# Attention and two MLPs on one core: q's sum and parts of the third and later head pairs tied to units 3 to 6 of the pair in front

## The chip, the cores and the metric

One core of a Trainium2 chip. The metric is device time of one execution in microseconds (us). Engines are named as in the profile: PE (TensorE matmul), PEld (its weight load), DVE (VectorE), ACT (ScalarE), POOL (GpSimd), SP (SyncE, which issues the DMAs). Each engine takes its instructions in the order in which they were laid down when the kernel was built. An instruction that waits holds up all that stand behind it on its engine.

## The reference

```python
# q, k, v: [4, 8, 576, 64] float32
def rotate(x):
    x1, x2 = (x[..., :half], x[..., half:])
    return np.concatenate([x1 * cos - x2 * sin, x1 * sin + x2 * cos], axis=-1)
q_rot, k_rot = (rotate(q), rotate(k))
scores = (1 / sqrt(64)) * np.matmul(q_rot, k_rot.transpose(0, 1, 3, 2))
scores = scores - np.max(scores, axis=-1, keepdims=True)
attn = np.exp(scores)
attn = attn / (np.sum(attn, axis=-1, keepdims=True) + 1e-09)
x = np.matmul(attn, v)               # turned to [2304, 512]
h = x @ w_in                         # [2304, 2048]
g = np.where(h >= 1, h, np.where(h <= -1, 0.0, (h + 1) ** 2 / 4))
x = g @ w_out                        # [2304, 512]
h = x @ moe2_w_in
out = (s * np.maximum(h, 0) ** 2 + b) @ moe2_w_out
```

## The kernel before

The four batches of eight heads are worked as 16 pairs of heads, counted here from 0 as in the code: pair i, i = 0 to 15. So the third pair of the title is pair 2. A pair has nine units, k = 0 to 8 (`UNITS`): eight are 128 query rows of one head, and unit 4 holds the last 64 rows of both heads. "Unit i.k" below is unit k of pair i, and n = 9i + k.

Numbers in full precision are multiplied as two parts, a high one that PE takes as it is and a low one that is what is left. For scores the high and low part of a head of q are stacked in the 128 rows of one tile (`qs`), and multiplied with two tiles of k, `kh` and `kz`.

One unit goes through the engines like this. PE makes the scores (`sc`, line 357), DVE takes the maximum of each row (`nm`, line 359), ACT takes the exponential and its sum (`p`, line 364), PE transposes it (`tp`, line 379), ACT or DVE copies that out of PSUM (`pt`, lines 382 to 386), and PE multiplies with v (`av`, line 405). There are two score buffers, so that PE can be two units ahead of the exponentials. `eb` (line 422, POOL) holds the inverses of the sums, which PE transposes (`rm`, line 433) and DVE multiplies in (`u`, line 441).

A pair's q needs five steps first: a load into a `qkin` tile (four of these, shared by q and k), a product with a table of cosines and sines on POOL (`pool_tt`, four pieces, line 96), a sum of its two halves on DVE (line 294), and then for each of the two heads the high part on ACT (line 308) and the low part on DVE (line 309). They end in `qs_t[i % 2]`, which the pair two in front has used. k goes the same way, with its sum on POOL, and is brought to `kh` and `kz` by six small DMAs (lines 326 and 329).

Beside the units run two more streams. The weights of the MLPs come in eight bytes a number and are converted on the chip, a half slice at a time, in one chain through ACT, DVE and POOL with one buffer for each step (`convert`: `wa` line 134, `wm` line 135, `wa` lines 137 and 138, `w` line 139, then two subtractions and two additions on POOL, line 96). From n = 48 on the first MLP of finished batches fills PE between the units (`run_fill`, the products `h` and `y`, line 181). What follows attention (the rest of the first MLP, then the second) is bound by PE.

The order on each engine is made when the kernel is built, by a scheduler that takes what is ready in the order of the program; `tc.issue_after(x)` keeps an instruction behind x. In `do_load`, q of pair i + 1 is asked for in unit i.0 as a whole, with no such tie from the third pair on. So its steps go as soon as their tiles are free and their data there, up to two pairs ahead. `maxs[n]` and `exps[n]` are the maximum and the exponential of unit n.

Of the kernel before, what the change touches and what calls it, by code (L numbers as in the profile page):

```python
# [14 lines left out]
ALU = mybir.AluOpType  # L15
# [51 lines left out]
def kernel(ctx, tc, qq, kk, vv, tab, ww1, ww2, s, b, out):  # L67
    nc = tc.nc
# [16 lines left out]
    def pool_tt(out, in0, in1, op, dim=-1):  # L85

        n = out.shape[dim]
        free = 1
        for x in out.shape[1:]:
            free *= x  # L90
        k = min(n, -(-free // PW))
        for i in range(k):
            c = [slice(None)] * len(out.shape)
            c[dim] = slice(n * i // k, n * (i + 1) // k)
            c = tuple(c)
            m = nc.gpsimd.tensor_tensor(out=out[c], in0=in0[c], in1=in1[c], op=op)  # L96
        return m
# [15 lines left out]
    exps, tps, maxs = {}, {}, {}  # L113

    class Slice:
# [6 lines left out]
        def convert(self, raw, pools, hi, lo):  # L122
            if not wide:
                split(hi, lo, raw, nc.scalar, nc.gpsimd)
                return


            top = raw.bitcast(F32).rearrange("p (n t) -> p n t", t=2)[:, :, 1]
            low = raw.bitcast(U16).rearrange("p (n t) -> p n t", t=4)[:, :, 1]
            pool = pools[self.f * 2 + self.made & 1 if len(pools) > 1 else 0]  # L130
            a = pool.tile([P, HW], F32, tag="wa", name="wa", bufs=WB)
            m = pool.tile([P, HW], F32, tag="wm", name="wm", bufs=WB)
            au, mu = a.bitcast(U32), m.bitcast(U32)
            nc.scalar.activation(a, top, AF.Copy, scale=2.0 ** -112)
            nc.vector.tensor_scalar(out=mu, in0=au, scalar1=3, scalar2=None, op0=ALU.logical_shift_left)
            nc.vector.scalar_tensor_tensor(out=mu, in0=au, scalar=0x80000000, in1=mu, op0=ALU.bitwise_and, op1=ALU.bitwise_or)
            nc.vector.tensor_scalar(out=au, in0=mu, scalar1=0xFF800000, scalar2=None, op0=ALU.bitwise_and)
            nc.vector.scalar_tensor_tensor(out=a, in0=low, scalar=2.0 ** -36, in1=a, op0=ALU.mult, op1=ALU.mult)
            nc.scalar.copy(hi, m)  # L139
            pool_tt(out=m, in0=m, in1=hi, op=ALU.subtract)  # L140
            pool_tt(out=lo, in0=m, in1=a, op=ALU.add)
# [106 lines left out]
    tab_sb = att.tile([P, 2, S], F32, name="tab_sb")  # L248
# [4 lines left out]
    qk_in, v_in, stacks = {}, {}, {}  # L253

    WHOLE = [slice(0, S)]
    HALVES = [slice(0, 288), slice(288, S)]

    def load_qk(i, nm, pieces=WHOLE):
        bb, hp = divmod(i, NP)
        t = att2.tile([P, 2, S], F32, tag="qkin", name=f"{nm}in", bufs=QB)  # L260
        for c in pieces:
            nc.sync.dma_start(out=t[:, :, c], in_=(qq if nm == "q" else kk)[bb, hp, :, :, c])
        qk_in[nm, i] = t

    def load_v(i):
        bb, hp = divmod(i, NP)
        t = att2.tile([P, 5, 2, D], F32, tag="vin", name="vin", bufs=VB)
        for out, src in ((t[:, :, 1], vv[bb, hp, :, :, 1]), (t[:D, :4, 0], vv[bb, hp, D:, :4, 0]), (t[D:, :4, 0], vv[bb, hp, :D, 1:, 0]), (t[D:, 4, 0], vv[bb, hp, :D, 0, 0])):
            nc.sync.dma_start(out=out, in_=src)
        v_in[i] = t  # L270
# [15 lines left out]
    def rope_pair(i, nm, mul, add, lo_eng, pieces=WHOLE):  # L286

        t = qk_in[nm, i]
        tt = {nc.gpsimd: pool_tt, nc.vector: nc.vector.tensor_tensor}
        last = None  # L290
        for c in pieces:
            tt[mul](out=t[:, :, c], in0=t[:, :, c], in1=tab_sb[:, :, c], op=ALU.mult)
            r = t[:, 1, c]
            tt[add](out=r, in0=t[:, 0, c], in1=r, op=ALU.add)
            last = (lay_q if nm == "q" else lay_k)(i, t, c, lo_eng)
        return last

    SELF = [slice(0, D), slice(D, P)]
    laid, parts = set(), {}

    def lay_q(i, t, c, lo_eng, heads=range(2)):

        st = stacks["q", i] = qs_t[i % 2]
        r = t[:, 1, c]
        for j in heads:
            own, other = SELF[j], SELF[1 - j]
            at = slice(j * QW + c.start, j * QW + c.stop)
            h = nc.scalar.activation(st[own, at], r[own], AF.Copy, scale=0.125)
            m = nc.vector.scalar_tensor_tensor(out=st[other, at], in0=r[own], scalar=0.125, in1=st[own, at], op0=ALU.mult, op1=ALU.subtract)
        return h.ins, m.ins  # L310
# [218 lines left out]
    def turned_by(t, c):  # L529
        nc.vector.tensor_tensor(out=t[:, :, c], in0=t[:, :, c], in1=tab_sb[:, :, c], op=ALU.mult)  # L530
        return nc.vector.tensor_tensor(out=t[:, 1, c], in0=t[:, 0, c], in1=t[:, 1, c], op=ALU.add).ins
# [53 lines left out]
    def do_load(n):  # L585
        if n == 0:
            with tc.issue_after(turned):
                turned_by(tq, QP[1])
                lay_q(0, tq, QP[1], None)
        elif n in (1, 2):  # L590
            with tc.issue_after(maxs[n]):
                if n == 1:
                    turned_by(tq, QP[2])
                else:
                    lay_q(0, tq, QP[2], None)
        if n < len(units):
            i, k = units[n]
            if i + 1 < NPAIR:
                if i == 0 and k in (2, 6):
                    with tc.issue_after(maxs[k]):  # L600
                        turned_by(qk_in["q", 1], HALVES[k // 6])
                if i == 0 and k in (4, 5, 7, 8):
                    with tc.issue_after(maxs[k]), tc.issue_after(exps[k - 1]):
                        lay_q(1, qk_in["q", 1], HALVES[k // 6], None, [int(k in (5, 8))])
                if i and k == 0:
                    with ExitStack() if i > 1 else tc.issue_after(parts[1][1]), ExitStack() if i > 1 else tc.issue_after(maxs[9]):
                        rope_pair(i + 1, "q", nc.gpsimd, nc.vector, None)
                elif k == 2:
                    with ExitStack() if i else tc.issue_after(exps[2]), ExitStack() if i else tc.issue_after(lowest):
                        rope_pair(i + 1, "k", nc.gpsimd, nc.gpsimd, [nc.gpsimd, nc.vector])  # L610
                elif k == 7:
                    load_v(i + 1)
                elif k in (4, 6) and i + 2 < NPAIR:
                    load_qk(i + 2, "q" if k == 4 else "k")

        if n in range(33, 51, 2) or n in range(70, 110, 4):
            with tc.issue_after(exps[n - 14]):
                convert()

        if n in PARK_AT and parking:  # L620
            with tc.issue_after(exps[n - 4]):
                parking.pop(0).park(wst, scratch)()
# [31 lines left out]
    def do_fill(n):  # L654
        if n < 48:
            return
        with tc.issue_after(exps[min(n, len(units)) - 4]):
            run_fill(0.62 if n < 76 else 0.92)

    acts = {"q": do_qk, "l": do_load, "t": do_t, "a": do_av, "f": do_fill}  # L660
    for n in range(len(units) + LA):
        with ExitStack() as st:
# [541 lines left out]
```

## Time and profile before

| | us |
|---|---|
| median of 3 runs | 1116.61 (1113.03 to 1118.2) |
| the profiled execution | 1117.65, its span 1115.9 |
| PE busy in the span | 1074.3 (96%) |
| DVE busy | 775.0 (69%) |
| ACT busy | 631.0 (57%) |
| POOL busy | 426.9 (38%) |

Attention lies between 9.08 us, where the first scores start, and 417 us, where the last maximum is taken. The shares are those of the whole span. In the first 140 us DVE and POOL are busy more than 80% of the time, so the shares of the attention stage, pair by pair, tell more.

### The profile page before, as it was taken

To read this page: it belongs to the slowest core of one execution; us is meant where nothing else is said; L and a number is where in the kernel's file an instruction comes from. 1 tells how busy PE (TensorE), PEld (TensorE's weight loads), DVE (VectorE), ACT (ScalarE), POOL (GpSimd) and SP (SyncE) were. 2 spreads that over 40 slices of the span, in tenths; PEclk is the share of its full clock that TensorE was granted. 3 is DMA by queue.
4 is the path that set the end of the run, shared out by engine and by line. 5 is a ranking of instruction groups with operands and counts; after the bars stand their busy time and mean duration, and the time that the engine had idled before them with its cause. 6 is when DMAs were issued, how large, how long until landed. Compare 5 with 4: busy or idle time off the path is not lost.

```text
span 1115.9 us, 20052 instructions
## 1 busy us (share of the span) xinstructions
PE 1074.3 (96%) x7296; PEld 981.3 (88%) x7296; DVE 775.0 (69%) x1445; ACT 631.0 (57%) x1440; POOL 426.9 (38%) x564
## 2 busy tenths in 40 slices
PE   5899999989999999999999999999999999999998
PEld 3666788878888889999999999999999999999997
DVE  7888987768576663454757667866777778677754
ACT  5777776766666665454545455474554448334431
POOL 6998977686473332332544445110212110000000
PEclk9999999999999999999999999999999999999999
DMA  8665856656675544655465673231322853221221
GB/s 240 168 191 167 253 160 208 207 165 188 202 227 166 174 151 138 220 171 190 149 183 203 211 238 116 86 112 59 113 89 90 301 171 116 82 83 42 80 63 36
DMA packets 109762, 173.24 MB, mean 155 GB/s; under 512 B 29408, under 2 KB 80608, under 8 KB 109664
## 3 DMA queue, kind: packets, MB, share of 16 engines
q1 hardware_dynamic: 109664, 171.97, 49.1%
q8 instruction: 57, 0.93, 0.4%
q14 instruction: 41, 0.34, 0.1%
HBM read 110.10 MB, written 48.56 MB: 142 GB/s over the span
## 4 chain that ended last, share of the span: by engine, by line
PE 81%; DVE 5%; DMA 5%; POOL 3%; ACT 3%; issue 2%; SPq 0%; POOLq 0%; ACTq 0%
PE hps L181 15%; PE sum L940 14%; PE yps L856 6%; PE yps L855 6%; PE yps L854 6%; PE y L181 5%; PE sc L357 5%; PE yps L790 4%; PE yps L791 4%; PE yps L792 4%; PE av L405 4%; PE h L181 4%; PE tp L379 3%; DMA wraw<-in_ww 1%; DMA kz<-kin 1%
## 5 line engine op out<-in xcount | busy, mean ns | idle before, releaser
L181 PE MATMUL hps<-xh,w 128*128 128x288 f32 (+4 forms) x640 | 163.4, 324 | 0.0
L357 PE MATMUL sc<-kh,qs 128*128 128x288 f32 x336 | 102.7, 328 | 24.5 <-ACT p L364 13.5
L359 DVE TENSOR_REDUCE nm<-sc 128x1 f32<-128x576 f32 x144 | 106.5, 748 | 24.9 <-PE sc L357 24.4
L364 ACT ACTIVATE p<-sc,nm 128x576 f32<-128x576 f32 x144 | 106.7, 742 | 28.6 <-DVE nm L359 26.2
L948 ACT ACTIVATE four<-four,b_sb,s_sb 128x480 f32<-128x480 f32 x64 | 47.4, 782 | 127.2 <-DVE four L947 127.2
L856 PE MATMUL yps<-gh,w 128*128 128x480 f32 (+1 forms) x320 | 118.5, 370 | 0.0
L854 PE MATMUL yps<-gh,w 128*128 128x480 f32 (+1 forms) x320 | 118.4, 370 | 0.0
L855 PE MATMUL yps<-gl,w 128*128 128x480 f32 (+1 forms) x320 | 118.4, 370 | 0.0
L96 POOL TENSOR_TENSOR wm<-wm,w 128x256 f32<-128x256 f32 x80 | 69.5, 888 | 119.1 <-ACT w L139 62.5
L181 PEld LDWEIGHTS hps<-xh,w 128*128 128x128 f32 x640 | 113.2, 188 | 1.0
L357 PEld LDWEIGHTS sc<-kh,qs 128*128 128x128 f32 x336 | 63.5, 192 | 45.7 <-ACT p L364 27.0
L181 PE MATMUL hps<-xl,w 128*128 128x288 f32 (+4 forms) x320 | 103.7, 324 | 0.0
L790 PE MATMUL yps<-gh,w 128*128 128x288 f32 (+3 forms) x288 | 93.2, 324 | 1.4 <-DVE yp L797 0.7
L357 PE MATMUL sc<-kz,qs 128*128 128x288 f32 x336 | 93.8, 301 | 0.0
L791 PE MATMUL yps<-gl,w 128*128 128x288 f32 (+3 forms) x288 | 92.8, 322 | 0.0
L792 PE MATMUL yps<-gh,w 128*128 128x288 f32 (+3 forms) x288 | 92.8, 322 | 0.0
L379 PE MATMUL tp<-ident,p 128*128 128x128 f32 x576 | 87.2, 276 | 4.0 <-DVE pt L386 3.4
L96 POOL TENSOR_TENSOR wm<-wm,raw 128x256 f32<-128x256 f32 x16 | 12.6, 806 | 176.8 <-ACT raw L139 176.8
L181 PE MATMUL y<-gh,w 128*128 128x288 f32 x320 | 75.0, 305 | 2.0 <-DVE ptr L397 0.9
L379 PEld LDWEIGHTS tp<-ident,p 128*128 128x128 f32 x576 | 70.5, 142 | 6.2 <-DVE pt L386 4.1
L405 PE MATMUL av<-pt,vin 128*64 128x256 f32 (+1 forms) x512 | 75.7, 417 | 0.0
L107 DVE TENSOR_TENSOR gl<-hps,gh 128x288 fp32r<-128x288 f32 (+4 forms) x88 | 46.4, 527 | 40.4 <-ACT gh L103 40.2
(154 smaller groups left out, 2905.9 us busy)
## 6 DMA issues: line engine op xcount, KB each, us to landing
wraw<-in_ww SPq DMA_DIRECT2D x56, 512.0 KB, 4.4
w<-parkd SPq DMA_DIRECT2D x24, 512.0 KB, 6.1
kin<-in_k SPq DMA_DIRECT2D x15, 576.0 KB, 4.4
qin<-in_q SPq DMA_DIRECT2D x15, 576.0 KB, 4.8
kh<-kin SPq DMA_DIRECT2D x60, 144.0 KB, 2.9
parkd<-wraw SPq DMA_DIRECT2D x16, 512.0 KB, 3.2
xs<-y1d SPq DMA_DIRECT2D x32, 240.0 KB, 2.7
xd<-u SPq DMA_DIRECT2D x16, 288.0 KB, 2.7
```

The costliest lines, as they stand in the source:

```text
L181: m = nc.tensor.matmul(out_ps, l, r, start=(i == 0), stop=(i == n - 1))
L357: nc.tensor.matmul(sc[:, half, o:o + n], l, r[:, k0:k0 + n], start=m == 0, stop=m == len(todo) - 1)
L364: exps[i * 9 + k] = nc.scalar.activation(p, sc[:, :, :288], AF.Exp, bias=nm, scale=1.0, accum_out=sums_t[i][:, col:col + 1]).ins
L379: m = nc.tensor.transpose(v[:, c, :], p[:, c * P:(c + 1) * P], ident)
L405: nc.tensor.matmul(ps[j * D:(j + 1) * D, :n], v[:, kt, j, :], pt[g][:, kt, j, :], start=kt == 0, stop=False)
L790: nc.tensor.matmul(acc, wh, gh, start=f == 0, stop=False)
L791: nc.tensor.matmul(acc, wh, gl, start=False, stop=False)
L792: nc.tensor.matmul(acc, wl, gh, start=False, stop=last)
L854: nc.tensor.matmul(acc, wh, gh, start=f == 0, stop=False)
L855: nc.tensor.matmul(acc, wh, gl, start=False, stop=False)
L856: nc.tensor.matmul(acc, wl, gh, start=False, stop=last)
L940: nc.tensor.matmul(acc, l, r, start=j == 0, stop=j == len(t) - 1)
```

## The change

From the third pair on, q is no longer prepared in one piece from unit i.0. The product on POOL stays at unit i.0 of the program, now without a tie. The sum on DVE comes at unit i.4, behind the maximum of unit i.3. The high and low part of the first head come at unit i.5, those of the second at i.6, each behind the maximum of the unit in front and the exponential of the unit before that. No instruction is added or taken away.

```diff
+                if i:
+                    t = qk_in["q", i + 1]
+                    if k == 0:
+                        with ExitStack() if i > 1 else tc.issue_after(parts[1][1]):
+                            pool_tt(out=t, in0=t, in1=tab_sb, op=ALU.mult)
+                    elif k == 4:
+                        with tc.issue_after(maxs[n - 1]):
+                            nc.vector.tensor_tensor(out=t[:, 1], in0=t[:, 0], in1=t[:, 1], op=ALU.add)
+                    elif k in (5, 6):
+                        with tc.issue_after(maxs[n - 1]), tc.issue_after(exps[n - 2]):
+                            lay_q(i + 1, t, WHOLE[0], None, [k - 5])
                 if i and k == 0:
-                    with ExitStack() if i > 1 else tc.issue_after(parts[1][1]), ExitStack() if i > 1 else tc.issue_after(maxs[9]):
-                        rope_pair(i + 1, "q", nc.gpsimd, nc.vector, None)
+                    pass
```

The scheduler makes another order on every engine in the attention stage from this. Three places are shown.

The first is DVE from the second maximum of pair 1 to its third and fourth. `qs_107` takes the low parts of pair 2; the second sum is that of pair 3. Before:

```order
L359 TENSOR_REDUCE nm<-sc 128x1
L386 COPY pt<-tp 128x4x128
L309 SCALAR_TENSOR_TENSOR qs_107<-qin,qs_107 64x576 x2
L294 TENSOR_TENSOR qin<-qin 128x576
L359 TENSOR_REDUCE nm<-sc 128x1
```

The same engine after, from the fourth maximum of pair 1 to the seventh:

```order
L359 TENSOR_REDUCE nm<-sc 128x1
L612 TENSOR_TENSOR qin<-qin 128x576
L386 COPY pt<-tp 128x4x128
L359 TENSOR_REDUCE nm<-sc 128x1
L309 SCALAR_TENSOR_TENSOR qs_107<-qin,qs_107 64x576
L359 TENSOR_REDUCE nm<-sc 128x1
L386 COPY pt<-tp 128x4x128
L309 SCALAR_TENSOR_TENSOR qs_107<-qin,qs_107 64x576
L420 RECIPROCAL sume<-sume 128x5
L359 TENSOR_REDUCE nm<-sc 128x1
```

Both low parts of pair 2 and the sum of pair 3 stood between two maxima. Now each step stands between two maxima of its own, and pair 3's sum stands in pair 2. In every later pair too, from 1 to 14, there is one sum behind the fourth maximum and one low part behind each of the next two. Before, pair 1 held two pairs' parts less one step and most later pairs held a sum for the pair three on and the low parts for the pair two on.

The second place is POOL at the second inverse of pair 2 (`eb`), where the second weight conversion (`wm_1084`, `w_1080`) is finished. `qin_1269` before and `qin_1265` after are q of pair 6, `kin_1327` is k of pair 6, `kin_1014` k of pair 5. Before:

```order
L422 COPY eb_882<-sume_879 128x256
L96 TENSOR_TENSOR wm_1084<-wm_1084,w_1080 128x256 x2
L96 TENSOR_TENSOR qin_1269<-qin_1269,tab_sb_106 128x2x144 x4
L96 TENSOR_TENSOR w_1080<-wm_1084,wa_1083 128x256
L96 TENSOR_TENSOR kin_1327<-kin_1327,tab_sb_106 128x2x144 x4
L96 TENSOR_TENSOR w_1080<-wm_1084,wa_1083 128x256
```

After:

```order
L96 TENSOR_TENSOR w_1080<-wm_1084,wa_1083 128x256 x2
L96 TENSOR_TENSOR kin_1014<-kin_1014 128x288 x2
L96 TENSOR_TENSOR qin_1265<-qin_1265,tab_sb_106 128x2x144 x4
L275 MEMSET vin_1056 64x64
L422 COPY eb_1045<-sume_1042 128x256
L275 MEMSET vin_1056 64x64
L96 TENSOR_TENSOR wm_1137<-wm_1137,w_1133 128x256 x2
L96 TENSOR_TENSOR w_1133<-wm_1137,wa_1136 128x256 x2
L96 TENSOR_TENSOR kin_1327<-kin_1327,tab_sb_106 128x2x144 x4
```

The conversion's last two additions stood behind the products of q and of k; now they stand in front of both, and the product of q is directly ahead of the first inverse of pair 3.

The third place is SP at the DMAs that bring k of pair 5 (`kin_1014`) to `kh` and `kz`. Before:

```order
L326 DMA kh_1199<-kin_1014 64x576 x4
L329 DMA kz1_110<-kin_1014 64x576 x2
L262 DMA qin_1595<-in_q 128x1152
L262 DMA kin_1641<-in_k 128x1152
L145 DMA wraw_1288<-in_ww1 128x512
```

After:

```order
L326 DMA kh_1194<-kin_1014 64x576 x4
L329 DMA kz1_110<-kin_1014 64x576 x2
L145 DMA wraw_1286<-in_ww1 128x512
L471 DMA xs_1564<-xd_57 128x288
L262 DMA qin_1591<-in_q 128x1152
```

The load of q for pair 7 (`qin_1595`, now `qin_1591`) stands a little further behind `kz`, and k's (`kin_1641`) went from directly behind it to the end of the same pair. Their tiles are swapped as well: because q's tile is given back later, q of pair i + 2 now takes the tile that k of pair i had (it waits for the DMAs that read it), and k takes q's.

## Rows read from the trace of the kernel before

**Rows 1.** Pairs 1, 2, 6, 9, all: length; busy PE, PEld, DVE, ACT, POOL; clock, DMA.
```profile
33.10:53.50 20.40, 17.31 (x125) 11.78 (x123) 17.75 (x27) 14.90 (x36) 18.63 (x24) 1.00 0.62 176
53.50:71.90 18.40, 18.08 (x133) 12.88 (x132) 16.02 (x28) 13.77 (x34) 16.54 (x21) 1.00 0.67 189
...
132.10:157.90 25.80, 23.24 (x168) 20.93 (x168) 20.73 (x37) 19.50 (x50) 22.11 (x31) 0.93 0.44 131
...
214.50:241.80 27.30, 23.55 (x182) 20.72 (x182) 20.16 (x37) 18.55 (x47) 20.21 (x28) 1.00 0.54 172
...
sum 384.00, PE 361.89 PEld 302.77 DVE 290.87 ACT 271.63 POOL 257.25; mean PE 24.13 PEld 20.18 DVE 19.39 ACT 18.11 POOL 17.15
```

**Rows 2.** Timeline of PE: start, duration, instruction, idle time before it and its releaser.
```profile
36.57 0.66 PE L379 MATMUL tp<-ident,p 128*128 128x128 f32 x4 [1.03 <-DVE pt L386]
...
41.42 0.40 PE L357 MATMUL sc<-kh,qs 128*128 128x288 f32 x1 [1.69 <-ACT p L364]
...
72.81 0.40 PE L357 MATMUL sc<-kh,qs 128*128 128x288 f32 x1 [1.23 <-ACT p L364]
...
104.09 0.44 PE L392 MATMUL tr<-ident,p 128*128 128x128 f32 x2 [0.70 <-DVE pt L386]
...
230.65 0.40 PE L181 MATMUL h<-xh,w 128*128 128x288 f32 x1 [1.33 <-ACT pt L384]
...
234.78 0.66 PE L379 MATMUL tp<-ident,p 128*128 128x128 f32 x4 [1.74 <-DVE pt L386]
```

**Rows 3.** Timeline of DVE at three of q's places.
```profile
36.54 2.02 DVE L309 SCALAR_TENSOR_TENSOR qs<-qin,qs 64x576 fp32r<-64x576 f32 x2
38.59 1.24 DVE L294 TENSOR_TENSOR qin<-qin 128x576 f32<-128x576 f32 x1
...
101.51 1.27 DVE L294 TENSOR_TENSOR qin<-qin 128x576 f32<-128x576 f32 x1 [1.88 <-POOL qin L96]
...
226.76 1.27 DVE L294 TENSOR_TENSOR qin<-qin 128x576 f32<-128x576 f32 x1 [3.45 <-POOL qin L96]
```

**Rows 4.** Groups of instructions, 28 to 440 us: count, busy, mean ns, idle before.
```profile
L309 DVE SCALAR_TENSOR_TENSOR qs<-qin,qs 64x576 fp32r<-64x576 f32 x28 | 25.3, 903 | 4.2 <-ACT qs L308 3.5
...
L294 DVE TENSOR_TENSOR qin<-qin x14: 879/1266/1345, 33.9 to 315.6; 128x576 f32<-128x576 f32 x14
...
L294 DVE TENSOR_TENSOR qin<-qin 128x576 f32<-128x576 f32 x14 | 16.5, 1180 | 12.4 <-POOL qin L96 12.3
...
L134 ACT ACTIVATE wa<-wraw 128x512 f32<-128x512 f32 x24 | 16.2, 674 | 16.0 <-POOL w L96 15.9
```

**Rows 5.** Timelines of POOL and of ACT around 70 us.
```profile
66.31 3.58 POOL L96 TENSOR_TENSOR kin<-kin,tab_sb 128x288 f32<-128x288 f32 x4
...
71.38 0.67 ACT L134 ACTIVATE wa<-wraw 128x512 f32<-128x512 f32 x1 [1.22 <-POOL w L96]
```

**Rows 6.** Busy time by engine and granted clock in pair 6, columns of Rows 1.
```profile
149.00:151.00 2.00, 1.00 (x9) 0.66 (x6) 2.00 (x5) 2.00 (x6) 1.43 (x2) 1.00 0.00 0
151.00:153.00 2.00, 1.12 (x7) 0.83 (x6) 2.00 (x5) 2.00 (x8) 2.00 (x4) 0.95 0.30 63
153.00:155.00 2.00, 2.00 (x10) 1.98 (x10) 1.36 (x4) 2.00 (x6) 2.00 (x3) 0.50 0.54 199
155.00:157.00 2.00, 2.00 (x13) 2.00 (x12) 1.05 (x2) 1.64 (x5) 2.00 (x3) 0.69 0.28 74
```

**Rows 7.** Timelines of SP and POOL in pair 4, and q's landing times.
```profile
94.06 0.55 SPq L262 DMA_DIRECT2D qin<-in_q  x1
95.91 0.34 SPq L262 DMA_DIRECT2D kin<-in_k  x1
...
98.41 3.07 POOL L96 TENSOR_TENSOR qin<-qin,tab_sb 128x288 f32<-128x288 f32 x4 [2.05 <-DMA qin<-in_q]
...
107.11 0.39 POOL L422 COPY eb<-sume 128x256 f32<-128x256 f32 x1
...
DMA to landing us min/median/max: 3.6/4.8/7.5
```

## The prediction on record

> **What bounds the kernel now.** I read the page's slices first: PE is busy nearly everywhere behind the attention stage, so that only attention can give time. Then I cut attention at the first maximum of each pair and asked for the busy time in each piece [rows 1]. The reader is to see three things there. Over pairs 1 to 15 PE is busy 361.89 of 384.00 us, so 22.1 us of idle PE are all that better order can win in this stage, apart from the clock. They lie unevenly: pair 2 has 0.32 us (18.40 less 18.08), pair 1 has 3.1, pair 6 has 2.6, pair 9 has 3.75. And DVE and POOL are close to PE in the early pairs (pair 1: 17.75 and 18.63 of 20.40), where nothing fills PE between the units, so that what is late on DVE is soon late on PE.
>
> Then I read which wait ends last, in the timeline of PE [rows 2]. PE waits for an exponential or for a copy out of PSUM, hardly ever for q itself. So q matters only as work that stands in front of maxima, copies and exponentials on engines that work in order.
>
> **What the change removes.** It takes no instruction away. In pairs 1 to 14 a sum at 1.18 us and two low parts at 0.90 us on DVE [rows 4], together 3.0 us, are placed anew, and before they had been spread over the pairs unevenly. I count where q's place can be tied to idle PE.
>
> Pair 1: two low parts of pair 2 (2.02 us) and the sum of pair 3 (1.24 us) run without a maximum between them [rows 3]. PE waits 1.03 us for a copy that DVE makes and 1.69 us for the exponential behind them [rows 2]. After the change one low part or one sum at a time stands between two maxima, and pair 3's sum leaves the pair. Removed: 2.72 us.
>
> Sums that wait for POOL: DVE stands idle in front of the sum for 12.3 us in all [rows 4], because the sum is laid directly behind its product, and the product itself waits for its load (2.05 us in pair 4) [rows 7]. Twice this reaches PE. The wait of 1.88 us at 101.51 [rows 3] is followed by 0.70 us of idle PE at 104.09; the wait of 3.45 us at 226.76 [rows 3] by 1.33 and 1.74 us at 230.65 and 234.78 [rows 2]. After the change a sum comes about two pairs after its product has been laid down on POOL's side, so that the product is long done. Removed: 3.77 us. The other waits of this kind are covered by the filling products on PE, and I count nothing for them.
>
> Conversions: when a conversion's additions stand behind a product of k (3.58 us at 66.31), ACT's next conversion step, which takes the same buffer, waits (1.22 us at 71.38) [rows 5] and holds the exponential behind it; PE then waits 1.23 us at 72.81 [rows 2]. ACT waits 15.9 us in all in this way [rows 4]. In the new order this conversion and the one that comes next have no product of q or k between their subtractions and additions. Removed: 1.23 us. In pair 6 it is a conversion with k's product of pair 9 between its halves; there PE is busy only 2.12 of the 4 us from 149 to 153 (1.88 us idle), and then the granted clock shows 0.50 and 0.69, the lower of its two levels (1.2 GHz) and a mix, in the next two stretches of 2 us [rows 6]. That costs 1.0 and 0.6 us more, with 0.1 us in the stretch before 1.7. In the new order k's product of pair 9 stands ahead of the subtractions. Removed: 3.58 us.
>
> Together 11.3 us.
>
> **What it adds.** The same 3.0 us of DVE and two high parts on ACT now stand in units 3 to 6 of every pair. No row shows that order, so I bound its price. The lower bound is the idle time of pair 2, 0.32 us: it already has one sum and two low parts, each between two maxima, and no wait for POOL [rows 1]. The upper bound is what pair 1 pays for three steps in one gap, 2.72 us. The new order is far nearer to pair 2, since no gap holds two of q's steps; but with a conversion's steps beside them some gaps are full, so I take 0.4 us. It is paid in pairs 1 to 11; from pair 12 on PE has filling work enough. 11 times 0.4 is 4.4 us. The lower bound gives 3.5 us.
>
> On SP the load of q now stands behind k's DMAs to `kz` and waits for their landing, because it takes k's old tile. In pair 4 that wait is what separates the load of k at 95.91 from that of q at 94.06 [rows 7]; q's load would go at about 96.7 us instead, with the two DMAs in between. Its product then starts at 101.1 instead of 98.41. Behind it on POOL stands the first inverse of the pair. In the trace this comes at 107.11 [rows 7]; after the change it comes at about 101.1 + 3.1 + 1.0 = 105.2 us (3.07 us is the product's length now, and 1.0 an estimate for the addition between them, from the 0.90 us of a quarter of the row of 3.58 [rows 5]). So I cost it at nothing: the inverse's own slack covers it, and a load that lands later than the median of 4.8 us, at the longest 7.5 us, still ends by 108. From that point on each us would be one of idle PE.
>
> The sum against the profiled execution: 1117.65 - 11.3 + 4.4 = 1110.7 us. The median of the runs shown lies 1.04 us under that execution, so I predict 1109.7 us.
>
> **A rule that speaks against it.** The sum of q takes between 0.879 and 1.345 us in the trace [rows 4], so something stretches it by up to 0.47 us. The Trainium skill (SBUF — State Buffer, Who interferes with whom) says that a DVE instruction with two inputs in SBUF and a GpSimd instruction that reads SBUF shut each other out for the whole instruction. By that rule each of q's three steps would wait out a piece of POOL's product.
>
> **The rivals.**
>
> *No change.* The idle time that goes is found again. PE in the pairs with filling work waits for many different things, and a new order makes new last waits; the conversions that I counted as undisturbed meet other products. Then only what DVE plainly does too much in pair 1 is won: 1117.65 - 2.7 = 1114.9, or 1113.9 on the median's scale. For it speaks that no single wait in pairs 2 to 11 has a share over a fifth of the 22.1 us. Against it, that both large events (pairs 6 and 9) show POOL's products of q or k at their head. Chance 0.27.
>
> *DVE and POOL shut each other out.* A piece of POOL's product takes 0.90 us (a quarter of 3.58) [rows 5]. If each of the three steps waited for a whole one, a pair would pay 2.7 us of DVE, less the 0.30 us by which the mean sum already exceeds the shortest, so 2.4. In pairs 1 to 5, where DVE is near its limit, this reaches PE: 12 us. 1117.65 - 6.9 + 12 = 1122.8 at the most; half the pieces met makes 1116.8, which is no change. The trace bears out half of the wait at most (0.47 of 0.90 us), and in the same way before the change. Chance 0.06. (It is the rule of the Trainium skill named above, in this kernel's numbers.)
>
> *Slower: the gap between two maxima.* In units 4 and 5 a copy, a low part, two conversion steps and a reciprocal may now stand between two maxima. PE can lead by two score buffers. If a gap outlasts that lead, each of pairs 1 to 11 pays as pair 1 paid, up to 2.72 us. The point from which this decides is (11.3 + 5.6) / 11 = 1.5 us per pair: above it the kernel is slower by more than 0.5%. At the full price it is 1117.65 - 11.3 + 29.9 = 1136; at 1.9 us it is 1127. Against it speaks pair 2, whose 0.32 us include such gaps; for it, that these units come with unit 4, which has more products on PE and so less spare DVE time later. Chance 0.17.
>
> **How the numbers follow.** My forecast has 0.50. 0.5% is 5.6 us, about what a measurement of this kernel can tell from no change, as its three runs lie within 5.2 us. The forecast's gain of 6.9 us exceeds this by little, so of its 0.50 I put 0.44 on faster and 0.06 on the same. With the two rivals that end near zero the same has 0.40 (0.06 + 0.27 + 0.06, and 0.01 of the last), slower has 0.16. The range: if all 11.3 us go and nothing comes back, the median's scale gives 1105.3; three runs lie up to 3.6 us under their median, so 1102. At the top it takes in no change, 1116.6, and the beginning of the third rival: 1119. The forecast's own range is 1105 to 1113.
>
> **What would show it.** In the changed kernel's trace: no idle DVE in front of the sum of q for POOL (12.3 us now); pair 1 shorter by 2 us or more; ACT's waits for POOL in front of `wa` under 10 us (15.9 now); no stretch at the lower clock near 155 us; PE idle in pairs 1 to 15 near 16 us. The prediction is wrong if PE's idle time stays near 22 us, with other releasers, or if the transposes of the inverses begin to wait for POOL.

## The result, and the profile after

The kernel before took 1115.83 us (median of 20 runs, 1111.22 to 1118.50), the changed one 1120.70 us (20 runs, 1116.95 to 1125.91). The ratio is 1.0051, 95% interval 1.004 to 1.0062: slower by an amount clear of noise, just at the 0.5% that the prediction took as its mark, where I had forecast 1109.7 us and a gain. The profiled run of the changed kernel, 1117.12 us with a span of 1115.3, is one of its lowest. In a second profile of it (1120.9 us, span 1119.1) PE is idle for 25.8 us in pairs 1 to 15, and the last maximum is taken at 421.5 us instead of 417.1. In the first it is taken at 417.0, as before. So the first profile shows where waits moved, and the loss itself stands in the second.

Pairs 1, 2, 3, 6, 7, 9 and the sum, first profile of the changed kernel, columns as in [rows 1]:

```profile
32.20:48.60 16.40, 16.40 (x123) 11.93 (x122) 13.31 (x24) 13.80 (x34) 14.80 (x21) 1.00 0.66 185
48.60:71.10 22.50, 19.98 (x135) 13.79 (x134) 17.50 (x29) 15.34 (x37) 16.30 (x22) 0.92 0.55 162
71.10:93.00 21.90, 18.65 (x136) 12.95 (x134) 17.36 (x30) 14.67 (x35) 17.65 (x24) 1.00 0.57 159
...
134.20:160.10 25.90, 22.32 (x159) 20.02 (x157) 20.99 (x37) 19.50 (x49) 21.86 (x29) 0.93 0.46 139
160.10:195.90 35.80, 32.75 (x242) 27.37 (x243) 24.14 (x45) 21.96 (x54) 25.43 (x35) 0.95 0.73 206
...
223.20:247.50 24.30, 20.57 (x156) 18.37 (x155) 22.24 (x42) 19.90 (x51) 19.37 (x25) 1.00 0.65 200
...
sum 384.80, PE 363.33 PEld 304.67 DVE 289.01 ACT 271.26 POOL 258.78; mean PE 24.22 PEld 20.31 DVE 19.27 ACT 18.08 POOL 17.25
```

Pair 1 is 4.0 us shorter than in [rows 1] and PE never idle in it. Pair 2 is 4.1 us longer, its idle PE 2.52 us instead of 0.32. PE's idle time over pairs 1 to 15 is 21.5 us, as before (22.1).

The groups that answer to [rows 4], with ACT's cast of k (line 321) beside them, 28 to 440 us:

```profile
L134 ACT ACTIVATE wa<-wraw 128x512 f32<-128x512 f32 x24 | 16.1, 670 | 6.1 <-POOL w L96 6.1
L612 DVE TENSOR_TENSOR qin<-qin 128x576 f32<-128x576 f32 x14 | 13.3, 949 | 0.2
L321 ACT CAST kin<-kin 128x576 fp32r<-128x576 f32 x14 | 9.4, 671 | 20.3 <-POOL kin L96 19.4 <-DMA xs<-xd 0.9
```

The sum no longer waits (0.2 us; 12.3 before) and takes 0.95 instead of 1.18 us. ACT waits less in front of `wa` (6.1; 15.9 before). But the cast of k, which waited 3.3 us for POOL before, now waits 19.4 (22.8 in the second profile). The same exchange stands in the waits of ACT, POOL and PE (us in total, times, longest). Before:

```profile
ACT kin L321 <- POOL kin L96: 3.3, 4, 1.2
POOL qin L96 <- DMA qin<-in_q: 22.5, 9, 8.1
POOL kin L96 <- DMA kin<-in_k: 0.6, 1, 0.6
...
PE sc L357 <- ACT p L364: 10.5, 14, 1.9
```

After:

```profile
POOL kin L96 <- DMA kin<-in_k: 29.8, 10, 6.3
POOL qin L96 <- DMA qin<-in_q: 4.4, 4, 1.8
...
PE sc L357 <- ACT p L364: 14.5, 14, 2.8
```

These lines name one inferred releaser each, and do not always name the load that landed just before. Added up from POOL's timeline, all its idle time directly in front of k's products is 1.1 us before, 29.8 after and 28.4 in the second profile (where the profile names the load for only 12.5), and in front of q's products 24.5 before and 14.2 after. PE waits for exponentials in the same number of waits, but longer.

In pair 2 of the kernel before, the load of k of pair 4, its product and its cast stand so:

```profile
44.46 0.33 SPq L262 DMA_DIRECT2D kin<-in_k  x1
...
48.55 0.80 POOL L96 TENSOR_TENSOR kin<-kin,tab_sb 128x288 f32<-128x288 f32 x1 [0.60 <-DMA kin<-in_k]
...
57.02 0.68 ACT L321 CAST kin<-kin 128x576 fp32r<-128x576 f32 x1
```

How a late load of k reaches PE is seen in the same pair of the changed kernel, in the timelines of SP, POOL, ACT and PE:

```profile
45.86 0.58 SPq L262 DMA_DIRECT2D kin<-in_k  x1
...
52.25 3.26 POOL L96 TENSOR_TENSOR kin<-kin,tab_sb 128x288 f32<-128x288 f32 x4 [2.74 <-DMA kin<-in_k]
55.48 1.25 POOL L96 TENSOR_TENSOR kin<-kin 128x288 f32<-128x288 f32 x1
...
57.03 1.30 POOL L96 TENSOR_TENSOR kin<-kin 128x288 f32<-128x288 f32 x1
...
58.37 0.67 ACT L321 CAST kin<-kin 128x576 fp32r<-128x576 f32 x1 [3.26 <-POOL kin L96]
58.94 0.61 ACT L139 CAST w<-wm 128x512 fp32r<-128x512 f32 x1
59.46 0.74 ACT L364 ACTIVATE p<-sc,nm 128x576 f32<-128x576 f32 x1
...
60.34 0.40 PE L357 MATMUL sc<-kh,qs 128*128 128x288 f32 x1 [1.80 <-ACT p L364]
```

POOL waits for the load, the two pieces of k's sum come late, ACT's cast stands waiting for them, and the exponential is behind the cast. PE stands still for 1.80 us. (In the second profile the cast waits 2.24 us here and PE 0.94 us.) From 60 to 64 us the granted clock is then 0.59, mostly its lower level. This load went out only 1.4 us later than before and took 6.3 us to land instead of 3.8, while pair 2 began 4.9 us earlier (48.6 instead of 53.5): here the shorter pair 1 does as much as the load to make k late. The loads of k for pairs 5 to 9 are issued 8 to 16 us later than before (59.70 to 67.69 us the first, 135.81 to 151.56 the last).

The second new place is pair 6, where I had said that a wait would go. These are the timelines of POOL, ACT and PE, and behind them stretches of 2 us at the new place, as in [rows 6]:

```profile
142.87 3.90 POOL L96 TENSOR_TENSOR qin<-qin,tab_sb 128x288 f32<-128x288 f32 x4 [1.80 <-issue]
146.73 2.02 POOL L96 TENSOR_TENSOR kin<-kin 128x288 fp32r<-128x288 f32 x2
...
148.80 1.85 POOL L96 TENSOR_TENSOR wm<-wm,w 128x256 f32<-128x256 f32 x2
...
150.94 1.86 POOL L96 TENSOR_TENSOR w<-wm,wa 128x256 fp32r<-128x256 f32 x2
...
152.83 0.66 ACT L134 ACTIVATE wa<-wraw 128x512 f32<-128x512 f32 x1 [1.88 <-POOL w L96]
...
154.27 0.40 PE L357 MATMUL sc<-kh,qs 128*128 128x288 f32 x1 [2.75 <-ACT p L364]
```

```profile
152.00:154.00 2.00, 0.00 (x0) 0.00 (x0) 0.48 (x2) 1.17 (x2) 1.14 (x3) 1.00 0.71 235
154.00:156.00 2.00, 1.06 (x6) 0.82 (x7) 2.00 (x5) 2.00 (x8) 0.76 (x2) 1.00 0.15 60
156.00:158.00 2.00, 2.00 (x11) 1.98 (x11) 1.97 (x4) 2.00 (x6) 2.00 (x4) 0.57 0.32 80
158.00:160.00 2.00, 2.00 (x9) 1.70 (x8) 1.69 (x4) 2.00 (x7) 2.00 (x3) 0.58 0.57 154
```

Now a product of q stands ahead of the conversion (its load went out at 139.00, behind k's DMAs to `kz`, and landed after 3.6 us, 0.3 us before the product starts), ACT's next conversion step waits as before, and PE is idle for the whole stretch from 152 to 154. The lower clock behind it takes 2 x (0.43 + 0.42) = 1.7 us, as much as before. The second profile has this wait again (2.74 us at 152.17).

The clock is the other part. Added up over stretches of 4 us from 28 to 444, the part below full clock is 1.7 us before and 5.1 us after (5.2 in the second profile). The 20 runs of the changed kernel had mean granted clocks of 0.989 to 0.995, median 0.9925; the profile before had 0.998, and the 97 runs of the kernel before beside the experiments 0.993 to 1.0, median 0.997. The two runs at 0.989 took 1124.62 and 1125.91 us, the three at 0.995 took 1117.12 to 1123.41.

### The profile page after: what moved, and what is told of

The parts are those of the page before. It is cut to its first block, busy times and chain, and to the rows that moved or that the text cites. A ratio compares the mean times of both kernels' runs of the same rounds, so it can differ in the third digit from the quotient of the medians.

```text
span 1115.3 us, 20036 instructions
## 1 busy us (share of the span) xinstructions
PE 1075.3 (96%) x7296; PEld 982.7 (88%) x7296; DVE 772.9 (69%) x1445; ACT 629.6 (56%) x1440; POOL 428.0 (38%) x564
## 4 chain that ended last, share of the span: by engine, by line
PE 82%; DMA 5%; DVE 4%; ACT 3%; POOL 3%; issue 2%; SPq 1%; POOLq 0%; ACTq 0%; DVEq 0%
PE hps L181 14%; PE sum L950 14%; PE yps L866 6%; PE yps L865 6%; PE yps L864 6%; PE sc L357 6%; PE h L181 5%; PE av L405 4%; PE y L181 4%; PE yps L800 4%; PE yps L801 4%; PE yps L802 4%; PE tp L379 4%; ACT p L364 1%; DMA qin<-in_q 1%
## 5 line engine op out<-in xcount | busy, mean ns | idle before, releaser
L364 ACT ACTIVATE p<-sc,nm 128x576 f32<-128x576 f32 x144 | 107.2, 745 | 28.3 <-DVE nm L359 25.8
```

Of the source, the lines that this page charges most:

```text
L364: exps[i * 9 + k] = nc.scalar.activation(p, sc[:, :, :288], AF.Exp, bias=nm, scale=1.0, accum_out=sums_t[i][:, col:col + 1]).ins
```

## The experiments

Three theories. **1, late loads:** q's tile is given back later, so a load comes late, POOL stands in front of its product, and k's sum, the conversions and, through ACT's queue, the exponentials are late. (For e1 to e4 it stood on record for k's load alone; the cast as its channel came in with e5, q's products and the conversions with e13.) **2, the gaps:** q's steps between the maxima of units 3 to 6 cost (my rival). **3, any new order** has such waits somewhere. All ratios are to the kernel before on the same chip, with 95% intervals.

### The loads by themselves

`e1_k_first` (on the changed kernel) and `e3_before_k_first` (on the kernel before):

```diff
-                    load_qk(i + 2, "q" if k == 4 else "k")
+                    load_qk(i + 2, "k" if k == 4 else "q")
```

`e2_before_k_late`, on the kernel before (`v_last[i]` is the last load of v of pair i):

```diff
+                    with tc.issue_after(v_last[i]) if k == 6 and i else ExitStack():
+                        load_qk(i + 2, "q" if k == 4 else "k")
```

`e4_sum_only`: the changed kernel with `lay_q(i + 1, t, WHOLE[0], None)` directly behind the sum, without ties.

> The changed kernel with the two loads exchanged: k of pair i + 2 is asked for in unit i.4 and takes k's old tile, q in unit i.6 and takes q's. All of q's steps stay tied as in the change. Theory 1 (k's late load is what costs: POOL stands in front of k's product until the load has landed, k's cast and the exponentials come late): POOL's wait for the load of k falls from 29.8 us to under 8, no single wait of PE over 2.5 us between 28 and 440 us, ratio to the kernel before 0.993 to 1.000 (1108 to 1116 us). Theory 2 (q's sum and low parts between the maxima of units 3 to 6 cost): these stand as in the change, so the ratio stays at 1.003 to 1.006 (about 1120 us). Theory 3 (no order as such costs, any new one bunches PE's waits somewhere and the clock drops): ratio anywhere from 0.998 to 1.006, and time follows the mean granted clock at about 1.1 us for 0.001.

> The kernel before, with nothing of q tied; only the load of k of pair i + 2 is kept behind the loads of v of pair i on SP, so that it stands where the change has put it. Theory 1: POOL waits for the load of k by 15 us or more (0.6 in the kernel before), ratio 1.003 to 1.007 (1119 to 1123 us). Theory 2: q's steps are where they were, so 0.999 to 1.001. Theory 3: 0.999 to 1.006 without a relation to k's wait.

> The kernel before with the two loads exchanged (k of pair i + 2 in unit i.4, q in i.6), nothing tied. Theory 1: k is as early as before or earlier, and q's product is the one that waits, so nothing that holds exponentials comes later: ratio 0.996 to 1.001. Theory 2: 0.999 to 1.001. Theory 3: 0.999 to 1.006.

> The changed kernel with only the sum tied (unit i.4, behind the maximum of unit i.3); the high and low parts follow it as soon as they can. k of the pair two on is loaded early in pairs 1 and 2 and late from pair 3 on. Theory 1: a part of the loss, ratio 1.002 to 1.005, POOL waits for the load of k by 10 us or more. Theory 2 (a step in each of three gaps costs; here both low parts share a gap with no order of their own): ratio 1.000 to 1.002. Theory 3: 0.999 to 1.006.

Measured: e1 1.0115 (1.0091 to 1.014), e2 1.0104 (1.008 to 1.0129), e3 1.0026 (1.001 to 1.0043), e4 1.0091 (1.0072 to 1.0111). In e2, POOL waits 26.4 us for loads of k (in all it stands idle 39.5 us in front of k's products, more than the 29.8 of the changed kernel):

```profile
POOL kin L96 <- DMA kin<-in_k: 26.4, 7, 6.6
```

So a late load of k costs with nothing of q tied, and theory 2 has no part in e2; the loss is above theory 1's range (1.003 to 1.007), and the edit moves other instructions too. e3 misses theory 1's range by a little: k's load was not early there, as I had thought, since POOL waits 17.9 us for it. And e1 falls far out of that range: k's load is asked for first, and the kernel is slower still. Its trace says why, on ACT and PE in pair 2:

```profile
67.81 0.67 ACT L321 CAST kin<-kin 128x576 fp32r<-128x576 f32 x1 [2.10 <-POOL kin L96]
...
70.13 0.61 PE L357 MATMUL sc<-kh,qs 128*128 128x288 f32 x1 [2.93 <-ACT p L364]
```

With the loads exchanged q's is the late one. POOL waits for both (22.0 us for q, 19.6 for k), k's sum behind them is as late as in the changed kernel, and ACT waits 19.6 us in front of the cast. So in both orders of the two loads one of them was late. e4 lies above the ranges of all three theories.

### The cast of k held back

`e5_cast_later` (changed kernel), `e6_before_cast_later` (before), `e7_k_first_cast_later` (e1); in `lay_k`, i is k's own pair:

```diff
-            cast = nc.scalar.copy(hi, r)
+            with tc.issue_after(exps[9 * i - 11]) if i > 1 else ExitStack():
+                cast = nc.scalar.copy(hi, r)
```

> The changed kernel with one tie more: ACT's cast of k (line 321) is kept behind the exponential of unit k = 7 of the pair two in front of its own, where POOL's sum is long done. Loads, tiles and q's ties as in the change. Theory 1 in its present form (what costs is that the cast of k stands on ACT in front of exponentials and waits there for POOL's late product and sum): ACT's wait in front of the cast falls from 19.4 us to under 4, the waits of PE for exponentials between 28 and 145 us from 7.6 to about 5, ratio to the kernel before 0.996 to 1.002, at least 0.3% below the changed kernel. Theory 2 (q's steps between the maxima cost) and theory 3 (any order has such waits; the clock follows them): the ratio stays at 1.003 to 1.007.

> The kernel before with the same tie of k's cast alone. Before, the cast waits for POOL by only 3.3 us. Theory 1: little to win, ratio 0.997 to 1.001. Theory 2: 1.000. Theory 3: 0.999 to 1.008, since other instructions on ACT, POOL and DVE move with it.

> The changed kernel with the loads exchanged (the first experiment, 1.0115) and the cast of k kept behind the exponential of unit k = 7 of the pair two in front. In the first experiment the cast waited for POOL by 19.6 us, and in pair 2 PE stood still for 2.93 us behind it, after which the clock was at its lower level. Theory 1: the ratio falls by 0.5% or more, to 1.006 or less. Theory 2 and theory 3: it stays at 1.008 to 1.014.

> The changed kernel once more, on the chip of the other runs of this group, as their yardstick and for a second profile: ratio 1.004 to 1.006 by every theory; the waits of PE for exponentials and POOL's wait for the load of k as in the first profile (29.8 us), and a mean granted clock of 0.990 to 0.995.

Measured: e5 1.0059 (1.0044 to 1.0074), e6 1.0064 (1.0042 to 1.0086), e7 1.0039 (1.0023 to 1.0055), the changed kernel again (e8) 1.0054 (1.0038 to 1.007). e7 against e1 shows the cast as a channel: 0.76% went when only the cast moved. In the changed kernel itself (e5) the cast's wait is gone too, and nothing is won: PE waits 8.1 us for exponentials between 28 and 145 us, where theory 1 had about 5 (7.6 without the edit), ACT waits 10.5 us in front of `wa` instead, and the time below full clock is 6.9 us. And in the kernel before the same tie costs 0.6%, which theory 1 had not expected: POOL now waits 21.0 us for the cast. The cast alone is not the cause.

### Part of the pairs, and a neutral edit

`e9_only_pair_2`, `e10_pairs_2_to_5` and `e11_pairs_6_on` are the changed kernel with its new part under `i == 1`, `1 <= i <= 4` or `i >= 5`, and the old `rope_pair` for the others. `e12_conversion_one_later` is the kernel before with

```diff
-            with tc.issue_after(exps[n - 14]):
+            with tc.issue_after(exps[n - 13]):
                 convert()
```

> The change made only for q of pair 2 (tied in pair 1); q of pair 3 and later as before. Pair 1 loses its crowding (two low parts and a sum in one gap), and only one load of k (pair 4) comes late. Theory 1 (late loads of k and what stands behind them on POOL and ACT cost, one pair at a time): pair 1 shorter by 2.5 to 4 us, half of that given back in pairs 2 and 3, ratio 0.997 to 1.000. Theory 3 (any new order bunches PE's waits somewhere, with the clock behind it): pair 1 shorter as well, ratio 1.001 to 1.006 with PE's idle time found in pairs that the edit did not touch.

> The change made for q of pairs 2 to 5 (tied in pairs 1 to 4), later pairs as before. Theory 1: the loss of pairs 2 and 3 stays (7.6 us longer in the profile of the changed kernel, 4.1 shorter in pair 1, 3.2 in pair 4), that of pairs 6 and 7 goes: ratio 1.001 to 1.004. Theory 3: 1.001 to 1.008.

> The change made for q of pair 6 and later (tied from pair 5 on), where products fill PE between the units; pairs 1 to 4 as before. Theory 1: pair 1 stays crowded, pairs 2 and 3 stay short, the late loads of k from pair 8 on meet filling work: ratio 0.998 to 1.003. Theory 3: 1.001 to 1.008, with one or two new stretches at the lower clock.

> The kernel before with an edit that has nothing to do with q or k: each weight conversion is kept behind the exponential one unit later (13 units back instead of 14). A few instructions of the conversions move on ACT, DVE, POOL and SP. Theory 1: 0.998 to 1.002, as no load of k is late. Theory 3 (the order before is one that happens to have few long waits, and most others have more): 1.002 to 1.008.

Measured: e9 1.0015 (0.9994 to 1.0037), e10 1.0121 (1.0089 to 1.0153), e11 1.0078 (1.0042 to 1.0114), e12 1.0014 (0.9993 to 1.0035). e12 and e9 show that a new order need not cost by being new. With one late load (e9) the loss is not to be told from none; with four or more it is there. But pair 1 of e9 took 20.2 us, 0.2 less than before and not the 2.5 to 4 expected; two sums of later pairs, which wait 1.25 and 1.16 us for POOL, still stand in it. And the parts do not add up to the whole: e10 alone loses twice what the change does, more than any theory had, and e11 is above theory 1's range. The longest wait of PE in e11 (5.66 us at 210.29) stands behind a stretched instruction of DVE, of which more below. What a late load costs seems to depend on what the order puts behind it; no run here separates that.

### q's product and the cast both later

`e13_q_product_later`: the changed kernel with q's product behind the low part of the same pair's k. `e14_q_product_and_cast_later`: that and the tie of e5. `e17_cast_two_units_behind`: e14 with `exps[9 * i - 10]`. `e16_both_later_untied`: both edits, but sum and parts by `rope_pair`, without ties.

```diff
-                    if k == 0:
-                        with ExitStack() if i > 1 else tc.issue_after(parts[1][1]):
+                    if k == 3:
+                        with tc.issue_after(parts[i + 1][1]):
                             pool_tt(out=t, in0=t, in1=tab_sb, op=ALU.mult)
```

`e15_sum_on_pool`: the changed kernel with the sum of unit 4 on POOL (`pool_tt`). `e18_sum_on_pool_cast_later`: that with the tie of e5.

> The changed kernel with q's product on POOL one pair later: behind the low part of the same pair's k, where its load has long landed; its sum and parts stay tied as in the change. Theory 1, as the traces of both profiles of the changed kernel now put it (POOL's products of q and k wait for loads that come late, and conversions, k's sum and through ACT's queue the exponentials wait behind them): the q product that starts at 142.87 us behind its load, 8 us before the conversion for which ACT then waits, starts without that wait; PE's 2.75 us at 154.27 fall under 1.5, the lower clock at 156 to 160 goes, ratio 1.000 to 1.003. Theory 2 (the sum and low parts in DVE's gaps between maxima; 5.7 us pass between two maxima at 141.59 and 147.25): nothing of DVE's moves, 1.004 to 1.007.

> The same, and the cast of k kept behind the exponential of unit k = 7 of the pair two in front as in the fifth experiment, so that neither ACT's cast nor q's product stands in a queue before its data are there. Theory 1: ratio 0.997 to 1.002. Theory 2: 1.004 to 1.007, with the longest waits of PE behind maxima that stand behind a sum or a low part.

> The changed kernel with q's sum on POOL in two pieces (as k's sum is), right behind its product, so that DVE has two steps of q in a pair instead of three; the low parts stay tied. POOL gets some 1.6 us more work in a pair. Theory 1: POOL's queue gets longer, ratio 1.004 to 1.010. Theory 2: DVE loses 1.18 us in each pair where gaps are full, ratio 1.002 or less.

> The kernel before (q's sum and parts without ties) with the two edits of the run that undid the loss: q's product on POOL behind the low part of the same pair's k, and the cast of k behind the exponential of unit k = 7 of the pair two in front. Sum and low parts follow the product at once, mostly all three between two maxima, so q's tile is given back nearly as late as in the change. If it is the two edits alone that win, whatever q's steps do on DVE: ratio 0.996 to 1.001. If q's three steps in one gap cost what I predicted of them (2.72 us in a pair with a crowded gap): 1.004 to 1.012, slower than with the ties (0.9994).

> The changed kernel with q's product one pair later and k's cast kept behind the exponential of unit k = 8, one unit later than in the run that gave 0.9994. Theory 1: it is the absence of waits at the head of the two queues that counts, not the one order that was hit: ratio 0.997 to 1.002. Theory 3 (a lucky order): 1.003 to 1.008.

> The changed kernel with q's sum on POOL (1.0066, of whose loss a 5.04 us wait of ACT's cast for POOL in pair 7 is the largest piece) and the cast of k kept behind the exponential of unit k = 7 of the pair two in front. Theory 1: ratio at most 1.002, and 0.996 if nothing takes the place of that wait, since the first six pairs of the run with the sum on POOL took 119 us against 125 before. If POOL's longer queue is what costs: 1.004 to 1.008.

Measured: e13 1.0066 (1.0043 to 1.0089), e14 0.9994 (0.9977 to 1.001), e15 1.0066 (1.0045 to 1.0086), e16 1.0056 (1.0036 to 1.0076), e17 1.009 (1.0072 to 1.0108), e18 1.0047 (1.003 to 1.0064).

With q's product out of the way (e13) the wait in pair 6 is gone as theory 1 expected (no wait of PE over 1.2 us in that pair), but the time does not fall. The casts hold PE longer than in the changed kernel, 2.08 us in pair 3 and 2.52 us in pair 4:

```profile
81.12 0.40 PE L357 MATMUL sc<-kh,qs 128*128 128x288 f32 x1 [2.08 <-ACT p L364]
...
101.29 0.40 PE L357 MATMUL sc<-kh,qs 128*128 128x288 f32 x1 [2.52 <-ACT p L364]
```

With both out of the way (e14) the loss is gone, with q's sum and parts where the change puts them. So these steps need not cost, which is against theory 2. Yet e17, one unit away, loses 0.9% again. Its worst place, in pair 5, is of another kind, seen here on DVE, POOL, ACT and PE:

```profile
117.16 3.54 DVE L613 TENSOR_TENSOR qin<-qin 128x576 f32<-128x576 f32 x1
...
116.82 1.56 POOL L96 TENSOR_TENSOR xl<-xs,xh 128x288 fp32r<-128x288 f32 x2
118.35 1.40 POOL L96 TENSOR_TENSOR wm<-wm,w 128x256 f32<-128x256 f32 x2
119.70 0.39 POOL L423 COPY eb<-sume 128x256 f32<-128x256 f32 x1
...
120.74 0.68 ACT L308 ACTIVATE qs<-qin 64x576 fp32r<-64x576 f32 x1 [2.74 <-DVE qin L613]
...
122.89 0.61 PE L358 MATMUL sc<-kh,qs 128*128 128x288 f32 x1 [4.04 <-ACT p L365]
```

The sum, 0.95 us in the mean of the changed kernel, takes 3.54 us beside an unbroken row of POOL's instructions. PE loses 4.04 us, and the clock from 120 to 128 us is 0.64 and 0.50. Its second longest wait, in pair 9, is theory 1's own: k's product waits for its load between the two additions of a conversion, ACT waits for the second addition, and the exponential stands behind.

```profile
219.74 3.05 POOL L96 TENSOR_TENSOR kin<-kin,tab_sb 128x288 f32<-128x288 f32 x4 [2.06 <-DMA kin<-in_k]
...
223.50 0.67 ACT L134 ACTIVATE wa<-wraw 128x512 f32<-128x512 f32 x1 [2.94 <-POOL w L96]
...
224.94 0.61 PE L358 MATMUL sc<-kh,qs 128*128 128x288 f32 x1 [3.82 <-ACT p L365]
```

e14 has the same place (PE waits 3.22 us at 216.93, its longest wait). So even e14 is not free of late loads of k: POOL stands idle 16.3 us in front of k's products there, and 22.5 us in e17. e16 has two places of the first kind, where an instruction of DVE lasts still longer; this is DVE in front of PE at 171.85 us, and POOL beside it:

```profile
164.99 5.16 DVE L135 TENSOR_SCALAR wm<-wa 128x512 uint32<-128x512 uint32 x1 [0.53 <-ACT wa L134]
170.17 0.76 DVE L360 TENSOR_REDUCE nm<-sc 128x1 f32<-128x576 f32 x1
...
164.21 1.58 POOL L96 TENSOR_TENSOR kin<-kin 128x288 fp32r<-128x288 f32 x2
165.73 3.05 POOL L96 TENSOR_TENSOR qin<-qin,tab_sb 128x288 f32<-128x288 f32 x4
168.72 0.80 POOL L96 TENSOR_TENSOR xl<-xs,xh 128x288 fp32r<-128x288 f32 x1
169.45 0.41 POOL L423 COPY eb<-sume 128x256 f32<-128x256 f32 x1
```

PE's wait there is 5.61 us. So e16's loss can't be put down to q's bunched steps alone, and e14 against e16 does not measure what the ties are worth.

e15 takes one step of q off DVE. Its pairs 1 to 6 take 119.3 us (127.9 in the changed kernel, 124.8 before), but pair 7 takes 44.4, where the converted weights come late; e18 shows the same, 120.5 and 40.1. The gain in the first pairs speaks for some truth in theory 2, but POOL's order changes with it, so it is not shown. No version beat the kernel before by more than its interval.

Taken together, POOL's idle time in front of k's products sorts the runs. It is 3.0 us or less in the kernel before, e6, e9 and e12, and 15.6 to 39.5 us in all others. Of the first group only e6 loses, and there POOL waits 21.0 us for the cast instead. Of the second all lose 0.26% or more but e14. So a loss and waits at the head of POOL's queue go together with one exception; how much is lost does not follow from their length (e13 33.3 us and 0.66%, e10 15.6 us and 1.21%). And by the medians the ranges of theory 1 held only in e7, e12, e14 and e15, besides the repeat e8; those of theory 3 held in e3, e5, e6, e9 and e11. Neither theory gives the size.

## Why the prediction was wrong

**The step that failed** is the one on SP, in "What it adds": "So I cost it at nothing". I followed the later load of q to its product and to one inverse behind it on POOL, and that part held, as far as its end: q's load went out at 97.27 us (about 96.7 predicted), and no wait of PE for `eb` appears, though the product starts at 104.74 and the inverse comes at 109.06 instead of 101.1 and 105.2, later than the 108 that I had taken for the limit. I did not follow k's load at all, although the change had swapped its tile too. Its load now waits for q's parts (as at 151.56 us, 0.03 us behind a low part) or stands behind those of v, POOL waits 29.8 us for it, and k's sum, ACT's cast and the exponentials stand behind (1.80 us of PE at 60.34). And I asked of q's later product only what inverse stood behind it, not what conversion did. e2 loses 1.04% with the load of k alone made late. That it is this load that costs the 0.5% of the change itself is argued from the trace: no run takes only its lateness away.

**The term that failed with it** is pair 6: "Removed: 3.58 us". I had seen in the order that k's product of pair 9 was no longer between the halves of a conversion; q's product came in its place, with a late load, and PE lost 2.75 us and the same 1.7 us of clock. The 1.23 us of pair 3 did go at their place, but 1.55 us at 82.48 came, behind the cast of k, which waits 3.12 us for POOL at 81.03.

**What held.** Pair 1: predicted 2.72 us, measured 4.0 us shorter (3.6 in the second profile). The sum's waits for POOL went from 12.3 to 0.2 us; but of the 3.77 us counted for them, pair 9's part did not come (idle PE 3.75 us before, 3.73 after). The waits in front of `wa` fell to 6.1 us, as I had said (under 10), but PE's idle time did not fall with it: the waits in front of the cast of k grew in the same queue, from 3.3 to 19.4 us.

**The gaps** (0.4 us a pair). One is seen: between the maxima at 141.59 and 147.25 stand the sum, a copy and four conversion steps, and ACT waits 2.21 us. Pairs 4 and 10 to 15 have no such price. That rival does not explain the loss: e14 has the same steps in the same gaps at 0.9994. **Port sharing**: in the two profiles of the changed kernel only one of DVE's instructions is stretched by more than 0.9 us (to 2.46 us at 350.09 in the second), so it did not decide there, but in eight of the experiments one or two are stretched by 2 to 5 us, and in e11, e16 and e17 PE's longest waits (5.66, 5.61 and 4.04 us) stand behind them. The chance of 0.06 that I gave this rival was for the change; in its neighbours it costs.

**The sum.** Of the idle PE that I counted, 4.5 us went in the first profile (pair 1 from 3.09 to 0, pair 4 from 2.09 to 0.70), and 4.1 us that I had not counted (pairs 10 to 15, from 4.8 to 0.8). It came back in pairs 2, 3, 5, 6, 7 and 8 (+2.2, +2.3, +0.7, +1.0, +1.1, +0.5), with 3.4 us more below full clock. In the second profile, where the loss stands, pairs 2, 3, 5, 6, 7, 8, 9 and 13 gave back more than the others won (+2.7, +1.0, +0.5, +1.5, +1.7, +1.5, +1.2, +2.0). My own test, idle PE near 22 us with other releasers, is what the profile shows.

**What stays open.** Which of the channels (cast, conversion) carries how much of the 0.5%: either edit alone wins nothing and both win it back, but with a late load of k still in place, and the neighbour of that order (e17) loses 0.9%, in part by a stretched instruction of DVE and in part by a late load. So e14 may be an order that happened to be good; no run here excludes it.

## What to carry to other kernels

Tying a step later gives its buffer back later. Follow each buffer of that pool to its next load, whoever's it is, and from the load through every queue in which its consumer stands in front of others. An instruction that has slack itself may still hold up those behind it. And look at the longest waits, not only at their sum: with 22.1 us of idle PE before and 21.5 in the first profile after, the waits of 1.2 us and more went from 7.9 to 10.3 us in all, and the time below full clock from 1.7 to 5.1. Not each long wait is followed by a lower clock: 1.55 us at 82.48 left it at 1.00.

## What the hardware did that I had not expected

DVE can be held far longer than one instruction of POOL's. In most places a stretched DVE instruction gains less than 0.9 us, one piece of POOL's product. But in e16 one of 0.4 us lasted from 164.99 to 170.15, until POOL's unbroken row of eight instructions from 164.21 on ended at 169.86; another took 5.42 us in e11, from 203.49 to 208.91, and there the row ended at 208.63. The Trainium skill (SBUF — State Buffer, Who interferes with whom) says that the engine that issues second is blocked for the whole instruction of the other. The long instructions here fit such blocking, but it lasts over several instructions of POOL, and the measurement decides.

The same order of instructions does not take the same time. Pair 1 has on every engine the order of the kernel before in e11 and e12, and took 22.9 and 25.1 us instead of 20.4. In e12 q's load came later, POOL waited 1.98 us for it, PE waited 3.17 us for an exponential instead of 1.69 [rows 2], and the clock was 0.63 in the stretch from 44 to 48 us.
